# New durations and due times for the planner of a fused attention and two-MoE kernel

## The chip, the core and the metric

The kernel runs on one core of a Trainium2 chip. The metric is the time of one execution on the device in microseconds (us), as the median of several runs. The core has five engines with a queue each, which work in the order of their own queue and wait for one another by semaphores: TensorE (PE, matrix products into PSUM), VectorE (DVE), ScalarE (ACT), GpSimd (POOL) and SyncE (SP), which here only issues DMA transfers.

## The reference

Three layers one after the other, all in float32.

```python
# 1. a linear attention with decay, batch 4, 8 heads, 768 positions, head 32, state 16, in chunks
L  = exp(cum[i] - cum[j]) * (i >= j)          # cum: running sum of log(a) in the chunk
y  = ((C @ B.T) * L) @ x + (C @ state) * exp(cum)
state = exp(cum[-1]) * state + sum_j B_j x_j exp(cum[-1] - cum_j)
x  = y.transpose(0, 2, 1, 3).reshape(3072, 256)
# 2. first MoE: 256 -> 1536 -> 256
xn = x / sqrt(mean(x*x) + 1e-6) * rms_g
x  = (silu(xn @ w_gate) * (xn @ w_val)) @ w_out
# 3. second MoE: 256 -> 1024 -> 256
h  = x @ w_in
s  = h * softmax(h)
x  = (s - mean(s)) / sqrt(var(s) + 1e-6) * g_ln @ w_out
```

## The kernel before

**Units and blocks.** The 3072 tokens are 24 units of 128, and six blocks (0 to 5) of four units each. Attention goes unit by unit, the first MoE block by block, the second MoE unit by unit. Weights come as 64-bit numbers and are turned into float32 on the chip: 26 pieces of 512 KB, each loaded (`wl`), put together by three VectorE operations (`wc`, lines 114, 117, 120), and split into a high half (`wh`, ScalarE, line 127) and a low half (`w`, line 131). Every large product runs as three matmuls on such halves (high by high, low by high, high by low).

**Names.** An operation is named by its kind and by its unit `u` or by its block and slice `b.f` (12 slices of the 1536 inner columns). For attention: `lpe` (decay by PE, first four units), `cb` (C times B), `mt` (times L), `bw` (B scaled), `y` (the product of the unit, line 358 on), `s2` and `sbd` (new state), `sq`, `ms`, `ts`, `pw`, `rb` (RMS norm), `xc`, `xn`, `xh`, `xl` (input of the first MoE in halves). First MoE: `gm` and `vm` (gate and value, line 622), `th`, `si`, `mu` (SiLU and product), `ah`, `al` (halves), `o0` and `o1` (product with w_out, line 664, two halves of the 256 outputs), `x2h` and `x2l` (lines 673, 677: the block's result in halves). Second MoE: `h` (line 473), `mx`, `ex`, `so` (softmax times h), `tr`, `ds`, `dl` (transposed on VectorE in 32x32 squares, stored to DRAM, loaded back as `tt`), `tc` and `tl` (halves `uth` and `utl`, lines 573 and 578), `f` (product with w_out, line 602), `out` and `st` (result scaled and stored). For units 20 to 23, the tail, PE transposes instead.

**The planner.** None of this is written in its final order. Each operation is declared by `op(name, engine, us, due, function, after, new, use)`: its engine, a duration, a due time, the operations that must come before it, and the buffers it takes. `plan()` (line 994 on) goes forward in a clock of its own: for each engine it estimates when each ready operation could start, lets those within `SLACK` of the earliest compete, and takes the one with the lowest due time. Operations with `alt` may move from VectorE to GpSimd. The order it ends with is the order of each engine's queue; the chip knows nothing of durations or due times. Buffers are rings (`BUFS`): an operation can't take one before its last user is done. The two banks of `hc` serve both `cb` and `h`, in turn.

**Due times.** `PRO` and `FIRST` say when block 0 starts and how long it lasts, `per1`, `perA`, `per2` how long the other blocks last per unit. From these come `start[b]`, the due times of the gate and value products, of attention (`Y0`, `YPOS`, `YSPAN`), of weights (`wdue`, `WGAP`) and of the second MoE (`HLAG`, `TAILGAP`).

Of the kernel before, what the change touches and what calls it, by code (L numbers as in the profile page):

```python
# [38 lines left out]
NPE = 4  # L39
MARGIN = {"PE": 0.5}  # L40
CROW = 30.0
WGAP = 8.0
HLAG = (50.0, 26.0)
# [7 lines left out]
def fused_kernel(ctx, tc, aT, xbt, bcT, wg, wv, wo1, rg, wi2, wo2, gl, consts, out):  # L51
# [606 lines left out]
    def o_mm(b, f, m):  # L658
# [4 lines left out]
        for i, (aa, ww) in enumerate(((d["ah"], wo1_s[0]), (d["al"], wo1_s[0]), (d["ah"], wo1_s[1]))):  # L663
# [40 lines left out]
    per1, perA, per2 = 12.4, 2.7, 6.5  # L704
# [15 lines left out]
    for i in range(26):  # L720
        t = wdue(i)
        kind, c = pieces[i][0]
        op(f"wl{i}", "SP", 0.45, EARLY[i] if i < len(EARLY) else t - 6, (w_load, i), after=[f"wl{i-1}"] if i else [], new=[("u", f"st{i}")], kb=512)
# [8 lines left out]
        op(f"wh{i}", "ACT", 0.63, t, (w_hi, i), after=[f"wc{i}.2"], use=[f"wt{i}"])  # L732
        op(f"w{i}", "DVE", 0.68, t, (w_lo, i, V), after=[f"wh{i}"], use=[f"wt{i}"], lock=True)
# [15 lines left out]
    for u in range(NU):  # L749
# [53 lines left out]
        if u >= SPLIT:  # L803
            op(f"cb{u}", "PE", 0.5, Y - 12.0, (at_cbr, u), after=cbok + Lok[1], new=[("hc", f"pcb{u}")],
# [30 lines left out]
    for b in range(NB):  # L835
# [3 lines left out]
        for f in range(NF):  # L839
# [12 lines left out]
            op(f"mu{s}", "DVE", v_us(N), t, (g_mul, b, f), after=[f"si{s}", f"vm{s}"], use=[f"th{s}", f"pv{s}"])  # L852
# [25 lines left out]
    for u in range(NU):  # L878
# [115 lines left out]
    def plan():  # L994
# [48 lines left out]
        while len(order) < len(ops):  # L1043
# [138 lines left out]
```

## Time and profile before

| | |
|---|---|
| median of 3 timed runs | 558.02 us (557.35 to 560.51) |
| the profiled execution | 554.45 us, span 552.6 us |
| mean granted TensorE clock | 0.981 |
| PE busy | 524.9 us (95%) |
| VectorE busy | 422.8 us (77%) |
| ScalarE busy | 309.5 us (56%) |
| GpSimd busy | 117.7 us (21%) |

The span runs from the first to the last instruction; 1.85 us lie around it. Matmuls overlap, so the busy time of PE also holds time in which it starts them more slowly than it could. An idle time matters only on the engine that sets the end of its stretch. The granted clock is a share of full speed: 1.00 is 2.4 GHz and about 0.5 is 1.2 GHz.

### The profile page before, as it was taken

The numbers are of one execution on the slowest core, as the hardware profiler recorded it, in microseconds if no ns is written. First come the engines' busy times: TensorE is split into PE (matmuls) and PEld (weight loads), VectorE is DVE, ScalarE is ACT, GpSimd is POOL, SyncE is SP. The second block draws the span as 40 slices with busy tenths as digits, with TensorE's granted clock in tenths as the row PEclk, the third lists the DMA queues.
The fourth block names the chain that finished last, engine by engine and source line by source line (L and its number), as shares of the span: only waits on it lengthen the run. The fifth ranks groups of instructions, "written<-read, shape, count | busy, mean of one in ns | idle before, by whom it ended". The sixth has DMA issues, their size and how long they took to land.

```text
span 552.6 us, 9279 instructions
## 1 busy us (share of the span) xinstructions
PE 524.9 (95%) x3240; PEld 438.2 (79%) x3240; DVE 422.8 (77%) x802; ACT 309.5 (56%) x670; POOL 117.7 (21%) x140
## 2 busy tenths in 40 slices
PE   8869998999999999999999999999999799999886
PEld 8847876777788888888888878878888688887786
DVE  4887999999996898778887878877875565375674
ACT  6526655565675675566674665765643343344455
POOL 1522443550320120424112212013302000010000
PEclk9868999999999999999999999999999899999999
DMA  5664755561174252363353264242221221022200
GB/s 169 182 194 148 232 186 187 180 191 57 46 219 144 86 178 91 105 185 108 104 167 105 80 184 134 92 148 93 56 86 49 77 79 55 11 76 87 85 21 28
DMA packets 44014, 65.00 MB, mean 118 GB/s; under 512 B 7360, under 2 KB 30272, under 8 KB 43968
## 3 DMA queue, kind: packets, MB, share of 16 engines
q1 hardware_dynamic: 43968, 64.42, 37.2%
q8 instruction: 25, 0.41, 0.3%
q14 instruction: 21, 0.17, 0.1%
HBM read 50.57 MB, written 13.83 MB: 117 GB/s over the span
## 4 chain that ended last, share of the span: by engine, by line
PE 64%; DVE 20%; DMA 7%; issue 4%; ACT 3%; SPq 2%; POOL 0%; DVEq 0%; ACTq 0%; POOLq 0%
PE pv L622 12%; PE pg L622 12%; PE po L664 11%; PE pf L602 11%; PE ph L473 10%; DMA xb<-in_xbt_dram 3%; DVE wt L117 3%; DVE wt L120 2%; DMA tt<-scr 2%; DVE th L644 2%; DVE th L640 2%; DVE al L656 2%; PE y L363 2%; DVE utl L578 2%; PE y L358 1%
## 5 line engine op out<-in xcount | busy, mean ns | idle before, releaser
L650 ACT ACTIVATE ah<-th 128x512 fp32r<-128x512 f32 x72 | 45.3, 629 | 61.9 <-PE po L664 38.2
L656 DVE TENSOR_TENSOR al<-th,ah 128x512 fp32r<-128x512 f32 x61 | 45.2, 740 | 25.7 <-ACT ah L650 25.4
L640 DVE SCALAR_TENSOR_TENSOR th<-th,pg 128x512 f32<-128x512 f32 x72 | 49.2, 684 | 18.5 <-ACT th L636 17.9
L622 PE MATMUL pg<-xh,wg_h 128*128 128x512 f32 x144 | 60.7, 421 | 2.7 <-DVE th L640 1.3
L664 PE MATMUL po<-ah,wo_h 128*128 128x512 f32 x144 | 58.9, 409 | 0.0
L664 PE MATMUL po<-al,wo_h 128*128 128x512 f32 x144 | 56.7, 393 | 2.2 <-DVE al L656 2.2
L622 PE MATMUL pv<-xh,wv_h 128*128 128x512 f32 x144 | 58.4, 406 | 0.2 <-DVE th L644 0.2
L622 PE MATMUL pg<-xl,wg_h 128*128 128x512 f32 x144 | 57.4, 399 | 0.4 <-DVE xl L442 0.4
L622 PE MATMUL pg<-xh,wg_l 128*128 128x512 f32 x144 | 57.0, 396 | 0.0
L622 PE MATMUL pv<-xl,wv_h 128*128 128x512 f32 x144 | 56.8, 394 | 0.0
L622 PE MATMUL pv<-xh,wv_l 128*128 128x512 f32 x144 | 56.8, 394 | 0.0
L664 PE MATMUL po<-ah,wo_l 128*128 128x512 f32 x144 | 56.7, 394 | 0.0
L602 PE MATMUL pf<-wo_h,utl 128*128 128x256 f32 x176 | 50.8, 289 | 5.4 <-DVE utl L578 5.4
L644 DVE TENSOR_TENSOR th<-pv,th 128x512 f32<-128x512 f32 x72 | 49.7, 690 | 7.0 <-PE pv L622 1.2
L602 PE MATMUL pf<-wo_h,uth 128*128 128x256 f32 x176 | 50.3, 286 | 4.1 <-ACT uth L573 4.1
L227 ACT ACTIVATE L<-L,cneg 128x128 f32<-128x128 f32 x160 | 50.5, 390 | 5.3 <-DMA L<-crow 5.1
L636 ACT ACTIVATE th<-pg 128x512 f32<-128x512 f32 x72 | 42.6, 592 | 17.8 <-PE pg L622 17.3
L602 PE MATMUL pf<-wo_l,uth 128*128 128x256 f32 x176 | 50.2, 285 | 0.0
L538 POOL TENSOR_TENSOR sc<-sc,mhalf 128x1 f32<-128x1 f32 x24 | 13.5, 564 | 169.3 <-DVE sc L533 165.2
L602 PEld LDWEIGHTS pf<-wo_h,utl 128*128 128x128 f32 x176 | 34.4, 195 | 7.4 <-DVE utl L578 6.7
L602 PEld LDWEIGHTS pf<-wo_h,uth 128*128 128x128 f32 x176 | 33.9, 192 | 5.7 <-ACT uth L573 5.0
L473 PE MATMUL ph<-wi_h,xh 128*128 128x512 f32 x96 | 37.9, 395 | 0.2 <-DVE L L298 0.2
(151 smaller groups left out, 1225.8 us busy)
## 6 DMA issues: line engine op xcount, KB each, us to landing
L<-crow SPq DMA_DIRECT2D x20, 512.0 KB
scr<-dt SPq DMA_DIRECT2D x20, 512.0 KB
tt<-scr SPq DMA_DIRECT2D x80, 128.0 KB
bc<-in_bcT_dram SPq DMA_DIRECT2D x48, 128.0 KB
stage<-in_wo_dram SPq DMA_DIRECT2D x10, 512.0 KB
xb<-in_xbt_dram SPq DMA_DIRECT2D x24, 192.0 KB
stage<-in_wg_dram SPq DMA_DIRECT2D x6, 512.0 KB
stage<-in_wv_dram SPq DMA_DIRECT2D x6, 512.0 KB
```

The lines of the kernel that those rows point to most:

```text
L117: V.scalar_tensor_tensor(out=t, in0=v[:, :, 1], scalar=-0x40000000, in1=t, op0=ALU.bitwise_and, op1=ALU.bitwise_or)
L227: A.activation(d["L"][:, h], d["L"][:, h], AF.Exp, bias=cneg[:, u * 8 + h:u * 8 + h + 1])
L473: T.matmul(ph[c], xx[:, kk, k * P:(k + 1) * P], ww[:, kk, 512 * c:512 * c + 512], start=(i == 0), stop=(i == 5))
L538: G.tensor_tensor(out=sc[:, 7:8], in0=sc[:, 6:7], in1=mhalf, op=ALU.pow)
L602: T.matmul(d["pf"][:, 0:DM], uu[:, k], ww[:, k], start=(k == 0 and i == 0), stop=(k == 7 and i == 2))
L622: T.matmul(ps[:, :n], ww[:, kk, f * P:(f + 1) * P], xx[:, kk, :n], start=(i == 0), stop=(i == 5))
L636: A.activation(d["th"], d["pg"], AF.Tanh, scale=0.5)
L640: V.scalar_tensor_tensor(out=d["th"], in0=d["th"], scalar=1.0, in1=d["pg"], op0=ALU.add, op1=ALU.mult)
L644: V.tensor_tensor(out=d["th"], in0=d["pv"], in1=d["th"], op=ALU.mult)
L650: A.activation(d["ah"], d["th"], AF.Copy)
L656: e.tensor_tensor(out=d["al"], in0=d["th"], in1=d["ah"].bitcast(F32), op=ALU.subtract)
L664: T.matmul(po[b, m][:, :n], ww[:, f, m * P:(m + 1) * P], aa, start=(f == 0 and i == 0), stop=(f == NF - 1 and i == 2))
```

## The change

It has three parts. The declared durations are set to other numbers (a few hundredths to a few tenths of a us each), and so is the planner's estimate of a DMA's end. An operation that moves to GpSimd is now entered under its new engine, so that what follows it on VectorE is estimated as waiting for it. And the due times change: those of blocks, attention (with an offset per block, `YO`), second MoE (offset `HO`), and weights, among them `LEAD`, by which loads are due 0.49 us after their piece instead of 6 before. The raw pieces of the first MoE's w_out (`wraw`) now lie in the space of the second MoE's w_out until that is filled. There is new code for blocks under `WIDE`; as `WIDE` is 0, no block takes it.

```diff
+LEAD = -0.49
+PER = (12.2, 2.89, 5.7)
+WIDE = 0
-PRO = 34.0
-FIRST = 63.0
+PRO = 30.4
+FIRST = 69.8
-Y0 = (9.0, 4.0)
-YPOS, YSPAN = 0.65, 1.0
-TAILGAP = 5.0
-SLACK = 0.1
-SLACK0 = 0.1
+Y0 = (8.6, 3.8)
+YPOS = 0.55
+YSPAN = 0.72
+TAILGAP = 1.67
+SLACK = 0.02
+SLACK0 = 0.0
-EARLY = (-1.0, 1.5, 4.0, 6.0)
+EARLY = (-1.0, 1.5, 4.0, 3.2)
-CROW = 30.0
-WGAP = 8.0
-HLAG = (50.0, 26.0)
+CROW = 43.0
+WGAP = 10.3
+HLAG = (36.3, 16.4)
+YO = (0.0, 15.1, 1.41, -3.1, 3.9)
+HO = (-0.73, 5.6, -11.1, 0.0, -2.51, 0.0)
...
-            V.scalar_tensor_tensor(out=t, in0=v[:, :, 0], scalar=29, in1=t, op0=ALU.logical_shift_right,
+            raw = w_raw(i) if pieces[i][0][0] == "o" else t
+            V.scalar_tensor_tensor(out=raw, in0=v[:, :, 0], scalar=29, in1=t, op0=ALU.logical_shift_right,
...
-    per1, perA, per2 = 12.4, 2.7, 6.5
+    per1, perA, per2 = PER
...
-        op(f"wl{i}", "SP", 0.45, EARLY[i] if i < len(EARLY) else t - 6, (w_load, i), after=[f"wl{i-1}"] if i else [], new=[("u", f"st{i}")], kb=512)
+        op(f"wl{i}", "SP", 0.45, EARLY[i] if i < len(EARLY) else t - LEAD, (w_load, i), after=[f"wl{i-1}"] if i else [], new=[("u", f"st{i}")], kb=512)
...
+            t = gdue(WIDE, 2 * c + LAG) - 8.0
...
-            Y = start[b - 1] + (k + YPOS) * (start[b] - start[b - 1]) / n * YSPAN
+            Y = start[b - 1] + (k + YPOS) * (start[b] - start[b - 1]) / n * YSPAN + YO[b - 1]
...
-        alt(f"bw{u}", 0.42, (at_bw, u, G))
+        alt(f"bw{u}", 0.57, (at_bw, u, G))
-                op(f"lpe{u}.{g}", "PE", 0.9, Y - 5, (at_lpe, u, g), new=[(tg, f"pl{u}.{g}")], use=[f"pl{u}.{g}"],
+                op(f"lpe{u}.{g}", "PE", 1.15, Y - 5, (at_lpe, u, g), new=[(tg, f"pl{u}.{g}")], use=[f"pl{u}.{g}"],
...
+        H += HO[b]
...
-            op(f"f{u}.3", "PE", mm_us(DM, 24), H + 1, (m_f4, u), after=[f"tl{u}.1"] + wout, new=[(tt[0], f"pf{u}")],
+            op(f"f{u}.3", "PE", 24 * 0.118, H + 1, (m_f4, u), after=[f"tl{u}.1"] + wout, new=[(tt[0], f"pf{u}")],
...
-                o = ops[nm] = dict(o, us=o["alt"][0], fn=o["alt"][1])
+                o = ops[nm] = dict(o, e=e, us=o["alt"][0], fn=o["alt"][1])
...
-                end[nm] = dma_free + 1.0
+                end[nm] = max(dma_free, t + o["us"] + 0.6) + 1.2
```

The order that comes out of it differs at many places. Three of them follow. PE at the startup, between C times B of unit 1 and that of unit 2 (`y_214` is unit 0, `y_292` unit 1; `pg` and `pv` are the two groups of unit 2's decay). Before:

```order
L398 MATMUL y_214<-ones_77,sq_247 128x1 x2
L249 MATMUL pg_266<-um_73,la_79 128x128 x4
L249 MATMUL pv_278<-um_73,la_79 128x128 x4
L358 MATMUL y_292<-cd_167,sbd_261 128x128 x2
L363 MATMUL y_292<-L_205,xb_164 32x128 x8
L368 MATMUL y_292<-xb_164 32x64 x4
L420 MATMUL y_214<-ident_74,r_272 128x128
```

And now:

```order
L268 MATMUL pg_260<-um_73,la_79 128x128 x4
L417 MATMUL y_214<-ones_77,sq_255 128x1 x2
L268 MATMUL pv_279<-um_73,la_79 128x128 x4
L377 MATMUL y_292<-cd_165,sbd_253 128x128 x2
L382 MATMUL y_292<-L_206,xb_143 32x128 x8
L387 MATMUL y_292<-xb_143 32x64 x4
L439 MATMUL y_214<-ident_74,r_286 128x128
```

The first decay group of unit 2 moved ahead of unit 0's sum of squares (`ms`).

VectorE at the end of block 4: `utl` is the low half for f of unit 14, `sc`, `ut` and `dt` behind the maximum (`TENSOR_REDUCE`) are those of unit 15, `xl` by line 677 is block 4's result. Before:

```order
L640 SCALAR_TENSOR_TENSOR th_4735<-th_4735,pg_4712 128x512
L644 TENSOR_TENSOR th_4735<-pv_4728,th_4735 128x512
L533 SCALAR_TENSOR_TENSOR sc_4692<-sc_4692 128x1
L411 TENSOR_SCALAR r_4754<-y_4697 128x1
L656 TENSOR_TENSOR al_4766<-th_4735,ah_4760 128x512
L484 TENSOR_REDUCE sc_4790<-ph_4768 128x1
L431 SCALAR_TENSOR_TENSOR xts_4724<-xts_4724,rgt_75,y_4697 128x128 x2
L677 SCALAR_TENSOR_TENSOR xl_4796<-po0_4132,xh_4795 128x512
L507 SCALAR_TENSOR_TENSOR ut_4800,sc_4790<-ph_4768,ut_4800 128x1024
L578 TENSOR_TENSOR utl_4804<-tt_4781,uth_4803 128x4x8x32
L442 TENSOR_TENSOR xl_4178<-xts_4724,xh_4177 128x2x128
L555 STREAM_TRANSPOSE dt_4811<-ut_4800 128x8x4x32
```

And now:

```order
L662 SCALAR_TENSOR_TENSOR th_4760<-th_4760,pg_4742 128x512
L669 TENSOR_TENSOR th_4760<-pv_4753,th_4760 128x512
L597 TENSOR_TENSOR utl_4764<-tt_4730,uth_4763 128x4x8x32
L681 TENSOR_TENSOR al_4789<-th_4760,ah_4787 128x512
L503 TENSOR_REDUCE sc_4816<-ph_4774 128x1
L526 SCALAR_TENSOR_TENSOR ut_4818,sc_4816<-ph_4774,ut_4818 128x1024
L574 STREAM_TRANSPOSE dt_4831<-ut_4818 128x8x4x32
```

The low half of unit 14 moved ahead of all of unit 15, and block 4's result behind it.

PE at the end of block 5 (`po` is block 5's last pair of o products, `pf` f of unit 18, `ph` h of unit 20). Before:

```order
L664 MATMUL po0_4912<-ah_5370,wo1_l_88 128x512
L664 MATMUL po1_4918<-ah_5370,wo1_h_87 128x512
L664 MATMUL po1_4918<-al_5375,wo1_h_87 128x512
L664 MATMUL po1_4918<-ah_5370,wo1_l_88 128x512
L602 MATMUL pf_5418<-wo2_h_91,uth_5409 128x256
L602 MATMUL pf_5418<-wo2_h_91,utl_5410 128x256
```

And now:

```order
L692 MATMUL po0_4921<-ah_5429,wo1_l_88 128x512
L692 MATMUL po1_4970<-ah_5429,wo1_h_87 128x512
L692 MATMUL po1_4970<-al_5434,wo1_h_87 128x512
L692 MATMUL po1_4970<-ah_5429,wo1_l_88 128x512
L492 MATMUL ph_5461<-wi2_h_89,xh_5448 128x512
L492 MATMUL ph_5461<-wi2_h_89,xl_5449 128x512
```

The product f of unit 18 left the place between the last o and h of unit 20; it now stands before the last three pairs of o.

## Rows read from the trace of the kernel before

**Rows 1.** Windows: from:to, length, busy us (instructions) per engine, PEclk, DMA.
```profile
core 0: us, PE busy (x) PEld busy (x) DVE busy (x) ACT busy (x) POOL busy (x), PEclk, DMA share, GB/s
0.00:38.20 38.20, 30.37 (x286) 26.92 (x286) 27.08 (x63) 19.38 (x54) 13.40 (x23) 0.86 0.59 167
38.20:107.00 68.80, 65.55 (x411) 51.36 (x411) 62.69 (x116) 39.52 (x99) 25.21 (x26) 0.96 0.60 190
107.00:182.00 75.00, 72.67 (x444) 58.47 (x443) 67.82 (x121) 47.72 (x109) 20.76 (x23) 1.00 0.43 134
182.00:431.00 249.00, 247.60 (x1510) 208.29 (x1511) 192.43 (x362) 149.35 (x313) 52.08 (x59) 1.00 0.37 116
436.00:446.00 10.00, 9.66 (x47) 8.75 (x48) 4.85 (x11) 2.95 (x5) 0.55 (x1) 0.83 0.36 119
500.00:552.60 52.60, 42.79 (x270) 37.64 (x268) 30.68 (x78) 25.42 (x51) 3.26 (x6) 1.00 0.17 58
```

**Rows 2.** Waits of PE over the span: us in total, times, longest.
```profile
PE pf L602 <- DVE utl L578: 5.4, 5, 2.3
PE pf L602 <- ACT uth L573: 4.1, 2, 2.1
```

**Rows 3.** Timeline of PE, startup: start, us, instruction [idle before it, released by].
```profile
16.56 0.63 PE L398 MATMUL y<-ones,sq 128*128 128x1 f32 x4 [1.63 <-ACT xts L426]
17.05 2.06 PE L249 MATMUL pg<-um,la 128*128 128x128 f32 x8
20.53 0.61 PE L358 MATMUL y<-cd,sbd 128*128 128x128 f32 x4
38.23 0.80 PE L622 MATMUL pg<-xh,wg_h 128*128 128x512 f32 x1 [1.21 <-ACT xh L438]
```

**Rows 4.** Timeline of VectorE, startup.
```profile
15.88 0.22 DVE L377 COPY s<-y 128x64 f32<-128x64 f32 x1
```

**Rows 5.** Chain of waits, block 4: start, us, piece of work.
```profile
391.72 1.39 PE pg L622 x6
...
394.47 2.72 PE ph L473 x12
397.19 2.82 PE pf L602 x24
400.01 1.40 PE po L664 x6
```

**Rows 6.** Timeline of PE, f of unit 14; last row from the chain.
```profile
434.88 0.38 PE L602 MATMUL pf<-wo_h,uth 128*128 128x256 f32 x1 [2.03 <-ACT uth L573]
436.33 0.38 PE L602 MATMUL pf<-wo_h,utl 128*128 128x256 f32 x1 [1.08 <-DVE utl L578]
...
436.33 4.51 PE pf L602 x23
```

**Rows 7.** Timeline, unit 17: last matmul of h, and `utl`.
```profile
480.58 0.39 PE L473 MATMUL ph<-wi_l,xh 128*128 128x512 f32 x1
...
494.13 1.22 DVE L578 TENSOR_TENSOR utl<-tt,uth 128x1024 fp32r<-128x1024 f32 x1
```

**Rows 8.** Timeline of ScalarE at the end of block 4.
```profile
432.19 0.60 ACT L673 ACTIVATE xh<-po 128x512 fp32r<-128x512 f32 x1 [4.27 <-PE po L664]
```

**Rows 9.** Timeline of PE, tail: f of units 18 (two rows), 19 and 23.
```profile
512.16 0.38 PE L602 MATMUL pf<-wo_h,uth 128*128 128x256 f32 x1 [2.10 <-ACT uth L573]
513.62 0.38 PE L602 MATMUL pf<-wo_h,utl 128*128 128x256 f32 x1 [1.08 <-DVE utl L578]
527.23 0.39 PE L602 MATMUL pf<-wo_h,utl 128*128 128x256 f32 x1 [2.34 <-DVE utl L578]
542.30 0.39 PE L602 MATMUL pf<-wo_h,xh 128*128 128x256 f32 x1 [0.97 <-DVE xl L592]
```

**Rows 10.** Groups by line: instruction, count, busy us, mean ns, idle before it.
```profile
L677 DVE SCALAR_TENSOR_TENSOR xl<-po,xh 128x512 fp32r<-128x512 f32 x12 | 8.1, 682 | 0.1
L673 ACT ACTIVATE xh<-po 128x512 fp32r<-128x512 f32 x12 | 7.1, 590 | 10.8 <-PE po L664 10.7
```

**Rows 11.** Waits of SyncE's queue: us in total, times, longest.
```profile
SPq L568 <- DMA scr<-dt: 20.0, 10, 2.7
```

More of the change, by code (lines that the diff above doesn't have):

```diff
@@ L179, in p_hi @@
     def p_hi(c):
+        if not wo2_s:
+            wo2_s.extend(wp.tile([P, 8, DM], F32R, name=f"wo2_{s}", bufs=1) for s in "hl")
         A.activation(wo2_s[0][:, 4 * c:4 * c + 4], w2[c], AF.Copy)
@@ L614, in fused_kernel, with awtag @@
     po = {}
+    def awtag(f):
+        return ("ah", "al")[f % 2]
     def g_mm(b, f, ws, tag):
@@ L662, in o_mm @@
         d = act[b, f]
-        for i, (aa, ww) in enumerate(((d["ah"], wo1_s[0]), (d["al"], wo1_s[0]), (d["ah"], wo1_s[1]))):
+        if b < WIDE:
+            T.matmul(po[b, m][:, :n], w_raw(3 * (f // 2) + 2).bitcast(F32)[:, 256 * (f % 2) + m * P:256 * (f % 2) + (m + 1) * P], d["aw"], start=f == 0,
+                     stop=f == NF - 1)
+        for i, (aa, ww) in enumerate(() if b < WIDE else ((d["ah"], wo1_s[0]), (d["al"], wo1_s[0]), (d["ah"], wo1_s[1]))):
             T.matmul(po[b, m][:, :n], ww[:, f, m * P:(m + 1) * P], aa,
@@ L731, in fused_kernel @@
             continue
-        op(f"wh{i}", "ACT", 0.63, t, (w_hi, i), after=[f"wc{i}.2"], use=[f"wt{i}"])
-        op(f"w{i}", "DVE", 0.68, t, (w_lo, i, V), after=[f"wh{i}"], use=[f"wt{i}"], lock=True)
+        wu = [f"wt{i}"]
+        last = []
+        if kind == "o":
+            t = gdue(WIDE, 2 * c + LAG) - 8.0
+            wu = [f"raw{c // 4}"]
+            ops[f"wc{i}.2"]["new"] += [(f"wo2_{'hl'[c // 4]}", wu[0])] if c % 4 == 0 else []
+            ops[f"wc{i}.2"]["use"] += wu
+            last = [f"o{m}{b}.{2 * c + q}" for b in range(WIDE) for q in range(2) for m in range(2)]
+        op(f"wh{i}", "ACT", 0.63, t, (w_hi, i), after=[f"wc{i}.2"], use=wu)
+        op(f"w{i}", "DVE", 0.68, t, (w_lo, i, V), after=[f"wh{i}"] + last, use=wu, lock=True)
         alt(f"w{i}", p_us(512), (w_lo, i, G))
@@ L740, in fused_kernel @@
         op(f"psub{c}", "DVE", 1.22, t, (p_sub, c), after=["pmean"], use=["mean"], lock=True)
-        op(f"phi{c}", "ACT", 1.06, t, (p_hi, c), after=[f"psub{c}"], use=["w2h", "w2l"])
+        op(f"phi{c}", "ACT", 1.06, t, (p_hi, c), after=[f"psub{c}"], use=["w2h", "w2l"],
+           new=[] if c else [("wo2_h", "w2H"), ("wo2_l", "w2L")])
         op(f"plo{c}", "DVE", 1.22, t, (p_lo, c), after=[f"phi{c}"], use=["w2h", "w2l"], lock=True)
@@ L803, in fused_kernel @@
         if u >= SPLIT:
-            op(f"cb{u}", "PE", 0.5, Y - 12.0, (at_cbr, u), after=cbok + Lok[1], new=[("hc", f"pcb{u}")],
+            op(f"cb{u}", "PE", 0.48, Y - 12.0, (at_cbr, u), after=cbok + Lok[1], new=[("hc", f"pcb{u}")],
                use=[f"bh{u}", f"cb{u}", f"pcb{u}"])
@@ L844, in fused_kernel @@
             wg_n, wv_n, wo_n = ([f"wh{3*(f//2)+q}", f"w{3*(f//2)+q}"] for q in range(3))
-            op(f"gm{s}", "PE", mm_us(N, 6), t, (g_gate, b, f), after=ready + wg_n + pr, new=[("pg", f"pg{s}")],
+            op(f"gm{s}", "PE", mm_us(N, 6) + 0.03, t, (g_gate, b, f), after=ready + wg_n + pr, new=[("pg", f"pg{s}")],
                use=[f"pg{s}", f"xs{b}"])
-            op(f"vm{s}", "PE", mm_us(N, 6), t, (g_val, b, f), after=[f"gm{s}"] + wv_n, new=[("pv", f"pv{s}")],
+            op(f"vm{s}", "PE", mm_us(N, 6) + 0.015, t, (g_val, b, f), after=[f"gm{s}"] + wv_n, new=[("pv", f"pv{s}")],
                use=[f"pv{s}", f"xs{b}"])
@@ L851, in fused_kernel @@
             op(f"si{s}", "DVE", v_us(N), t, (g_silu, b, f), after=[f"th{s}"], use=[f"th{s}", f"pg{s}"])
-            op(f"mu{s}", "DVE", v_us(N), t, (g_mul, b, f), after=[f"si{s}", f"vm{s}"], use=[f"th{s}", f"pv{s}"])
+            wide = b < WIDE
+            op(f"mu{s}", "DVE", v_us(N), t, (g_mul, b, f), after=[f"si{s}", f"vm{s}"], new=[(awtag(f), f"aw{s}")] if wide else [],
+               use=[f"th{s}", f"pv{s}"] + ([f"aw{s}"] if wide else []))
+            for m in range(2) if wide else ():
+                op(f"o{m}{s}", "PE", mm_us(N, 4), to, (o_mm, b, f, m), after=[f"mu{s}", f"wc{3*(f//2)+2}.2"] + ([f"o{m}{b}.{f-1}"] if f else []) + ([f"o0{s}"] if m else []),
+                   new=[(f"po{m}", f"po{m}{b}")] if f == 0 else [], use=[f"aw{s}", f"po{m}{b}", f"raw{f // 8}"])
+            if wide:
+                continue
             op(f"ah{s}", "ACT", a_us(N, 0.02), t + 2, (g_ah, b, f), after=[f"mu{s}"], new=[("ah", f"ah{s}")],
@@ L891, in fused_kernel @@
         if not tl:
-            op(f"h{u}.1", "PE", mm_us(512, 12), H, (m_h2, u), after=x2ok + win, new=[("hc", f"ph{u}")],
+            op(f"h{u}.1", "PE", mm_us(512, 12) + 0.02, H, (m_h2, u), after=x2ok + win, new=[("hc", f"ph{u}")],
                use=[f"ph{u}", f"x2{b}"])
```

38 lines of the change are left out of this document (25 added, 13 removed).

## The prediction
> **What bounds the kernel now.** I read the stretches first [rows 1]: the reader is to look at the first two numbers of each row, its length and TensorE's (PE's) busy time. From 182 to 431 us PE is busy 247.60 of 249.00 us: there only PE counts, and an order can win 1.4 us at most. Elsewhere PE stands: 7.8 us of the first 38.2, 3.3 of the next 68.8 (block 0, where VectorE is busy 62.69 us too), 2.3 up to 182, 9.8 of the last 52.6. Next, for whom PE waits [rows 2]: 5.4 us for the low and 4.1 us for the high half of the transposed activations of the second MoE (`utl`, `uth`), the operands of its last product f. Both kernels issue the same matmuls, so the change can only add or remove waits, and time at half clock behind them.
>
> **Startup (0 to 38.2 us), -2.4 us.** In [rows 3] the product ms of unit 0 sits until 16.56, since ScalarE's copy comes after VectorE's state copy s2, which only ran at 15.88 [rows 4] behind weight conversions. Queued behind ms on PE are the two groups of unit 2's decay product; they then take from 17.05 to 20.53, 3.5 us, and unit 1's y starts at 20.53. The changed order puts the first of these groups ahead of ms and gives unit 1's B scaling, which stood ahead of s2, to GpSimd. So that group starts as soon as PE is free, 1.6 us of wait (16.56's row) is filled with it, and y can start when VectorE is ready, some 3 us sooner. Not all of that arrives at the first gate matmul (38.23): VectorE does more before y of unit 3 (one low half of the weights and a state mask that GpSimd did, unit 1's `xl`), and the last `xl` stands behind three small operations instead of one. Ends: -4 (all of it and 1 us of the later waits), +0.5 (all lost on VectorE). I take -2.4, nearest the 3 us that the row shows. The slow clock of the first gate products (0.96 is the mean granted over block 0 [rows 1], 1.00 later) stays: they still follow a startup full of waits.
>
> **Block 0 and the first half of block 1 (38 to 182), -2.5 us.** Here conversions, gate and value all want VectorE. By counts of its instructions times their median durations, block 0 holds the same VectorE work in both orders; only places move. The second products o come one step later, which spares waits such as 2.2 us for one `al`. PE's idle time, 3.3 and 2.3 us [rows 1], is the most that goes; the same amount may come if VectorE falls behind at another place. I take -2.0 and -0.5; ends -5.6 and +5.
>
> **Blocks 2 to 4 (182 to 431), 0.** Ends -1.4 (all idle time) and +4 (below, the slower rival).
>
> **Unit 14, at the end of block 4 (432 to 441), -4.6 us.** What a matmul group costs is in [rows 5]: gate, value and a pair of o products 1.4 each, h 2.72, f 2.82. What unit 14 waited for is in [rows 6]: PE sat 2.03 us for `uth` and 1.08 for `utl`, and behind that f ran its 23 matmuls in 4.51 us against 2.82 for 24: 1.69 us, at a granted clock of 0.83 over 436 to 446 [rows 1]. Sum 4.8. The transposition takes its time whatever happens: in unit 17, where nothing stood in its way, 14.4 us from the end of the last h matmul (480.97) to the end of `utl` (495.35) [rows 7]. For unit 14 the old order leaves PE only four pairs of o (5.6), one gate and value (2.8) and h of unit 15 (2.7): 11.1 us and one small y. ScalarE was no help: it sat 4.27 us behind the copy of block 4's result, which waits for o [rows 8], with `uth` queued behind it. In the new order, between h and f of unit 14 lie f of 13 (2.82), three gates and values (8.25), three pairs of o (4.2) and h of 15 (2.72): 18.0 us, and VectorE has `utl` ahead of unit 15's maximum, where it stood behind its maximum, product and `xl` (second excerpt). 18.0 against 14.4 to 17 leaves nothing to wait for. I take -4.6; it is 0 if the chain grows to 21 us.
>
> **Tail (500 to the end), -4.0 us.** PE waits in [rows 9]: f of 18 2.10 and 1.08, f of 19 2.34, f of 23 0.97. Unit 18 had f of 17 (2.82), a gate and value (2.75), four pairs of o (5.6), h of 19 (2.72): 13.9 us; it gets 18.0. Unit 19's `utl` is now ahead of unit 21's maxima on VectorE and its `uth` no longer behind unit 18's. So 5.5 us go. But in the old order f of 18 lay between the last o and h of unit 20, and now nothing does (third excerpt): PE stands until ScalarE and VectorE have copied block 5's result, 0.59 + 0.68 us [rows 10] and about 0.2 for handing over, 1.5 us. That wait is bounded by 0.7 (first half only) and 3.0 (with a clock loss like unit 14's). It also gives unit 19 room: 2.82 + 4.2 + 1.5 + 8.2 (three units' h) = 16.7 us before its f. The last 0.97 I leave. -5.5 + 1.5 = -4.0; ends -6.5 and -1.
>
> **A rule against this.** After unit 14's waits the clock fell (0.83), after unit 18's, 3.18 us in all, the stretch stayed at 1.00 [rows 1, 9]. The Trainium skill, "TensorE: Matmul & The Clock Gate", section "HAM oscillation — how this bites in real kernels", says that gaps in TensorE's work send it back to half rate, so that what follows starts cold. The trace agrees in one of two like places. By the rule the new wait before h of 20 costs its 1.5 us and a cold start; by the row of unit 18 the 1.5 alone.
>
> **The sum.** -2.4 - 2.5 + 0 - 4.6 - 4.0 = -13.5. The profiled execution took 554.45 us (span 552.6), so 541.0 for its like. The three timed runs have a median of 558.02, 3.6 above it; carried over: **544.5 us**.
>
> **Rivals.**
> 1. *The waits only move.* Startup and block 0 are held by VectorE, which has the same work, and the f waits partly reappear before h of 20 and f of 22. Then unit 14's 4.6 us alone go: 553.4. For it: VectorE's 62.69 busy us of 68.8 in block 0. Against: the f of 14 and 18 now have more PE work before them than the chain takes.
> 2. *It does not do what it says.* Same work, same PE bound for 249 of 552 us; gains and new waits cancel: 556 to 560. For it: in 249 of the 552 us PE is busy but for 1.4. Against: the 9.5 us of [rows 2] lie outside that stretch.
> 3. *Cold after the new wait.* As forecast, but h of 20 starts at half clock (price 1.7, unit 14's row): 546. This is the rule above as a mechanism of this kernel; PE fell to half clock in one of two such waits.
> 4. *Slower: SyncE's queue in blocks 2 to 4.* The transposition goes out and back through SyncE, in order. The new order puts other transfers and the store of the unit before, which waits for that unit's f, ahead of the load back. If the load of each of the 14 units 6 to 19 leaves 2 us later, the distances of 17 to 20 us no longer hold a chain that takes 14.4 at its best, and each f waits about 1.5: +21 us on the 544.5 gives 565. It decides from 1 us a unit, where the gain is gone. For it: SyncE waited 20.0 us in 10 loads back for the store before them, 2.7 at the longest [rows 11]. Against: the old order, too, has the store of the unit before in that place, and PE still lost only 1.4 us in these blocks.
>
> **How the numbers follow.** Forecast 0.55, rival 3 0.12, rival 1 0.19, rival 2 0.08, rival 4 0.06. "Faster" means under 555.2, "slower" over 560.8 (0.5%, about what a measurement can tell from no change). Faster: 0.55 + 0.12 + 0.19 = 0.86; same 0.08; slower 0.06. The forecast's own range, from about half of each part's ends, is 538 to 551. Range 536 to 555: below, all gains at their ends (-4 - 5.6 - 1.4 - 4.8 - 6.5 = -22 gives 536); above, rival 1 with a little more lost.
>
> **What would show it.** Right: no wait of PE for `uth` or `utl` over 1 us in units 14, 18 and 19; one new wait of `ph` for `xl` of about 1.5 us before unit 20; the first gate matmul near 36; the 0.83 after 436 gone. The startup step is wrong if the first gate matmul starts after 38; the unit 14 and tail steps if f still waits; block 0 if it takes over 69 us from the first gate matmul to block 1's. The forecast as a whole falls if PE's idle time between block 2 and block 4 grows beyond 4 us.

## The result, and the profile after

The changed kernel takes 542.70 us (median of 4 runs, 542.03 to 542.93), the kernel before 557.98 (557.35 to 560.51): ratio 0.9716, 95% interval 0.9685 to 0.9747. The forecast was 544.5. Profiled executions: 554.45 before, 542.93 after, span 541.2.

To compare the two orders at the same work, I took for each operation on TensorE (PE) its start, less the durations that all groups before it have when nothing waits [rows 5]: that is the time PE has lost so far. The difference of the two kernels' lost time, by stretch:

| stretch (us, before) | forecast | measured |
|---|---|---|
| startup, to the first gate product | -2.4 | -0.6 |
| 38 to 182 | -2.5 | +2.1 |
| blocks 2 to 4 | 0 | -2.8 |
| unit 14 | -4.6 | -5.2 |
| tail | -4.0 | -5.0 |
| sum | -13.5 | -11.5 |

The windows of the changed kernel, as [rows 1]:

```profile
0.00:37.65 37.65, 29.83 (x287) 26.29 (x287) 26.50 (x65) 19.43 (x54) 13.66 (x21) 0.87 0.59 171
37.65:108.10 70.45, 67.14 (x407) 52.03 (x407) 64.90 (x117) 39.34 (x101) 20.30 (x21) 0.92 0.59 191
108.10:182.00 73.90, 72.08 (x438) 58.33 (x439) 71.32 (x129) 45.95 (x106) 18.94 (x20) 1.00 0.36 114
182.00:431.00 249.00, 248.95 (x1537) 210.91 (x1536) 191.87 (x358) 152.56 (x319) 51.34 (x65) 1.00 0.38 121
436.00:446.00 10.00, 10.00 (x46) 8.13 (x45) 6.56 (x9) 4.20 (x7) 0.28 (x1) 1.00 0.18 54
490.00:541.20 51.20, 46.56 (x283) 40.27 (x281) 30.70 (x75) 24.91 (x51) 2.74 (x5) 0.99 0.14 47
```

From 182 to 431 us PE stands for 0.05 us where it stood for 1.4, and the stretch after 436 has its full clock (0.83 before). Block 0 is longer (70.45 against 68.8) at a lower clock (0.92 against 0.96), with VectorE busy 2.2 us longer and GpSimd 4.9 us less.

Waits of PE over the span, as [rows 2]: us in total, times, longest.

```profile
PE y L439 <- POOL r L435: 2.3, 1, 2.3
PE pg L644 <- DVE wg_l L148: 2.0, 2, 1.4
PE pg L644 <- DVE th L662: 1.8, 3, 1.3
...
PE pg L644 <- ACT xh L457: 1.5, 1, 1.5
...
PE ph L492 <- ACT xh L701: 0.4, 1, 0.4
PE pf L621 <- DVE utl L597: 0.4, 1, 0.4
PE ph L492 <- DVE xl L705: 0.2, 1, 0.2
```

The 9.5 us for `uth` and `utl` are down to 0.4, and the new wait before h of 20 (`ph` for `xh` and `xl` of block 5) is 0.6. What is left at the top are waits of the startup and of blocks 0 and 1. Unit 14, from the chain of waits, as [rows 6]:

```profile
425.89 2.77 PE ph L492 x12
428.67 2.82 PE pf L621 x24
431.49 1.39 PE pg L644 x6
```

f of 14 follows h of 15 at once and takes its 2.82. SyncE's queue waited for the store before a load back about as often as before [rows 11], and from 182 to 431 us it cost PE nothing (0.05 us of idle time):

```profile
SPq L587 <- DMA scr<-dt: 21.6, 12, 3.5
```

### The profile page after: what moved, and what is told of

It is laid out like the page before. It is cut to its first block, busy times and chain, and to the rows that moved or that the text cites. A ratio compares the mean times of both kernels' runs of the same rounds, so it can differ in the third digit from the quotient of the medians.

```text
span 541.2 us, 9289 instructions
## 1 busy us (share of the span) xinstructions
PE 523.6 (97%) x3240; PEld 437.6 (81%) x3240; DVE 424.5 (78%) x806; ACT 308.3 (57%) x670; POOL 109.2 (20%) x136
## 4 chain that ended last, share of the span: by engine, by line
PE 85%; DVE 10%; issue 2%; ACT 1%; DMA 1%; SPq 0%; POOL 0%; DVEq 0%; ACTq 0%; POOLq 0%
PE pg L644 17%; PE pv L644 17%; PE po L692 16%; PE pf L621 13%; PE ph L492 12%; PE y L382 2%; PE pcb L310 2%; PE y L377 1%; DVE wt L128 1%; PE pcb L362 1%; DVE L L320 1%; DMA bc<-in_bcT_dram 1%; PE y L417 1%; DVE wt L131 1%; DVE th L662 1%
## 5 line engine op out<-in xcount | busy, mean ns | idle before, releaser
L681 DVE TENSOR_TENSOR al<-th,ah 128x512 fp32r<-128x512 f32 x60 | 41.7, 695 | 19.8 <-ACT ah L675 19.5
L621 PE MATMUL pf<-wo_h,utl 128*128 128x256 f32 x176 | 49.6, 282 | 0.4 <-DVE utl L597 0.4
L516 ACT ACTIVATE ut<-ph,sc 128x1024 f32<-128x1024 f32 x20 | 22.3, 1114 | 34.3 <-DVE sc L503 34.3
L250 POOL TENSOR_SCALAR_AFFINE_SELECT L<-L 128x1024 f32<-128x1024 f32 x20 | 23.0, 1148 | 83.7 <-ACT L L246 73.9
```

Source lines behind the costliest of these rows:

```text
L250: G.affine_select(out=d["L"], in_=d["L"], pattern=[[0, 8], [1, P]], base=0, channel_multiplier=-1, compare_op=ALU.is_ge, fill=0.0)
L516: A.activation(d["u"], ph[0], AF.Exp, bias=sc[:, 0:1], accum_out=sc[:, 1:2])
L621: T.matmul(d["pf"][:, 0:DM], uu[:, k], ww[:, k], start=(k == 0 and i == 0), stop=(k == 7 and i == 2))
L681: e.tensor_tensor(out=d["al"], in0=d["th"], in1=d["ah"].bitcast(F32), op=ALU.subtract)
```

## The experiments

But for the three that change the planner, each kernel is the one before or the changed one, with a helper behind `plan()` that moves the named operations to another place in their own engine's queue (in 11 and 12 some low halves to GpSimd's) and leaves the rest. The indented text under an edit is what was expected before the run.

**1. Unit 14 by distance alone (from the kernel before).**

```diff
+("f14.3", "after", "vm5.1"), ("h16.1", "after", "f14.3"), ("f15.3", "after", "o15.1"),
+("th5.1", "before", "tc15.1"), ("out14", "after", "th5.1"),
+("si5.1", "before", "mx16.0"), ("mu5.1", "before", "mx16.0")
```

> The kernel before, with nothing but unit 14's distance on TensorE changed: f of 14 moves behind two more gates and values (5.5 us), h of 16 behind it, f of 15 behind one more gate, value and pair of o; ScalarE and VectorE are moved only so far that nothing waits in a circle. Theory A (distance is what unit 14 lacked): f of 14 no longer waits (2.03 and 1.08 before), no half clock behind it (1.69), block 4 to 5 shorter by 4.8, time 553.2 (552.5 to 554). Theory B (the wait only moves, as the new place of f lets the load back of unit 15 stand where f of 15 needs it): f of 15 waits for 2 to 3 us instead, 556 to 557.

565.54 (561.7 to 567.62, ratio 1.0125, 1.0086 to 1.0165): slower than either theory allows. f of 14 does not wait any more, but the first gate product of block 5, now ahead of it, does. PE and ScalarE in this run:

```profile
435.51 0.49 PE L622 MATMUL pg<-xh,wg_h 128*128 128x512 f32 x1 [2.34 <-ACT xh L438]
437.00 0.50 PE L622 MATMUL pg<-xl,wg_h 128*128 128x512 f32 x1 [1.00 <-DVE xl L442]
```

```profile
432.52 0.60 ACT L673 ACTIVATE xh<-po 128x512 fp32r<-128x512 f32 x1 [4.27 <-PE po L664]
434.10 1.05 ACT L573 ACTIVATE uth<-tt 128x1024 fp32r<-128x1024 f32 x1
435.05 0.41 ACT L438 ACTIVATE xh<-xts 128x256 fp32r<-128x256 f32 x1
```

`xh` of unit 23 stands behind block 4's copy on ScalarE, as `uth` does. The old wait for `uth` had covered that. So distance on PE is not enough: whatever PE does instead must not need what is queued behind that copy. More was lost later, behind the moves of this experiment itself: 1.84 us for an `ah` behind `uth` of 15 and 3.04 for a `th` behind a variance. So the 565.54 is not the price of distance alone.

**2. Unit 14 by the queues alone (from the kernel before).**

```diff
+("tc14.1", "before", "x2h4.0"), ("tl14.1", "before", "mx15.0")
```

> The kernel before, with TensorE's order kept, and only the two halves of unit 14 moved up: uth ahead of the copy of block 4's result on ScalarE, utl ahead of unit 15's maximum on VectorE. The load back of unit 14 landed at about 432.2, so uth ends at 433.4 and utl at 434.6, 1.7 earlier. Theory A (distance): f of 14 still waits, about 0.6 and 1.0, so -1.7, or -3.4 if the clock stays up; 554.6 to 556.3. Theory B (the places on ScalarE and VectorE were the whole cause): no wait is left, -4.8, 553.2. Theory C (unit 15's maximum, now 3 us later, costs what unit 14 gains): 557.5 to 559.

555.73 (ratio 0.9951, 0.9924 to 0.9977): -2.6, within theory A. PE at f of 14 and the gate product behind it:

```profile
431.12 0.38 PE L602 MATMUL pf<-wo_h,uth 128*128 128x256 f32 x1 [0.34 <-ACT uth L573]
432.38 0.38 PE L602 MATMUL pf<-wo_h,utl 128*128 128x256 f32 x1 [0.88 <-DVE utl L578]
...
436.35 0.50 PE L622 MATMUL pg<-xl,wg_h 128*128 128x512 f32 x1 [0.78 <-DVE xl L442]
```

2.0 us of wait stay, since the distance is still 11 us, and nothing runs at half clock behind them (granted 1.00 from 429 to 440 us). f of unit 15, which did not wait before, now waits 0.65 us for its `utl`, so a part of theory C came too. The queues alone give about half of what unit 14 lost; the distance alone, as it was moved in experiment 1, only moved the wait.

**3. f of unit 18 back as a cover (from the changed kernel).**

```diff
+("f18.3", "after", "o15.11"), ("out18", "after", "x2h5.1"), ("st18o", "after", "dl19"),
+("ah5.11", "before", "ex19.0"), ("al5.11", "before", "mx19.0")
```

> The changed kernel, with f of unit 18 back in its old place, between the last o product and h of unit 20 (its result's copy and store behind block 5's copy and unit 19's load back; the halves ah and al of the last slice ahead of unit 19's maximum, so that o needn't wait for them). Theory A (the new wait before h of 20 costs what the sum said, 1.5, or what the trace of the changed kernel shows, 0.4 + 0.2 idle and about 0.6 of slower matmuls): f covers the copy and 0.6 to 1.5 go, 541.2 to 542.1 against 542.7. Theory B (the wait moves: h of 19 to utl of 19 is a chain of its own): f of 19 waits for utl longer by what h of 20 won, 542.5 to 543.

546.32 (ratio 0.9768, 0.9741 to 0.9794), 3.6 above the changed kernel: both theories fall. The trace, PE at h of 20, then ScalarE:

```profile
509.86 0.60 PE L492 MATMUL ph<-wi_h,xh 128*128 128x512 f32 x1 [2.45 <-ACT xh L701]
```

```profile
508.08 1.15 ACT L543 ACTIVATE ut<-ut,sc 128x1024 f32<-128x1024 f32 x1 [2.62 <-DVE sc L538]
509.23 1.06 ACT L701 ACTIVATE xh<-po 128x512 fp32r<-128x512 f32 x2
```

Block 5's copy does not wait for o (its last product ended at 504.58) but stands behind unit 19's variance (L543), which waits for unit 19's chain on VectorE. That chain runs later here, because the experiment also moved `ah` and `al` of the last slice ahead of it (the exponential of unit 19 starts at 504.26, in the changed kernel at 500.75); so the run says nothing of f of 18 as a cover by itself. In the changed kernel the variance (505.17 to 506.32) happens to end as o does (506.56). The copy was named rightly as what h of 20 waits for, and wrongly as waiting for o alone.

**4 to 6. The change taken apart.** The changed kernel with the old due times, constants and slacks (`durations`); with the old durations, DMA estimate and counting (`due`); the kernel before with the counting alone (`count`):

```diff
-                o = ops[nm] = dict(o, us=o["alt"][0], fn=o["alt"][1])
+                o = ops[nm] = dict(o, e=e, us=o["alt"][0], fn=o["alt"][1])
```

> The changed kernel with all due times, their constants and slacks as before; what stays of the change are the declared durations, the estimate of a DMA's end, the counting of moved operations and the place of the raw w_out pieces. In the order that comes out, between h and f of unit 14 lie 18.3 us of TensorE work (12.8 before, 18.4 in the changed kernel), with uth and utl behind block 4's copy as before; units 18 and 19 keep 13.9 and 12.6; the decay group stands ahead of unit 0's mean of squares. Theory A (a wait goes where its own distance grows): unit 14's 4.6 and the startup's 0.6 go, the tail's waits stay: about 553 against 558. Theory B (distance alone moves the wait, as in the run with spacing alone): 557 to 562. Theory C (the durations carry the whole gain): 543 to 546.

560.70 (ratio 1.0034, 1.0001 to 1.0067). At unit 14 f does not wait, although `uth` and `utl` stand behind block 4's copy as before; PE waits 0.45 us for `xl` of unit 23 and loses 1.0 in all instead of 5.4. Here `xh` of unit 23 had also come ahead of block 4's copy, which is what experiment 1 lacked. The tail's waits for f of 18 stayed, with a clock of 0.77 from 515 to 530 us. And before block 1 PE sat, at a granted clock of 0.71 from 105 to 118 us:

```profile
113.47 1.01 PE L417 MATMUL y<-ones,sq 128*128 128x1 f32 x4 [4.38 <-DVE s L398]
...
117.29 0.79 PE L644 MATMUL pg<-xh,wg_h 128*128 128x512 f32 x1 [1.39 <-ACT xh L457]
```

Theory A reads the two places rightly and the time wrongly.

> The changed kernel with the declared durations, the estimate of a DMA's end and the counting of moved operations as before; what stays are the due times, their constants and slacks, and the place of the raw pieces. In its order unit 14 has 16.8 us between h and f, with utl ahead of most of unit 15's work, unit 18 has 23.6, unit 19 has 12.6; the startup on TensorE is the old one. Theory A (places at the block ends carry the gain, whatever the durations): unit 14's 4.6 and unit 18's 3.2 go, unit 19 still waits 2 to 3: 548 to 551. Theory B (due times only fit the new durations): 554 to 560.

548.02 (ratio 0.9797, 0.9772 to 0.9823), as theory A has it, though f of 19 waited only 0.37 us. So the due times alone bring 10.4 of the 15.3 us; the durations alone, with the DMA estimate and the counting, lose 2.3, and on top of the due times they bring 5.3. The place of the raw pieces was the new one in both runs; none parted it.

> The kernel before with one line of the change: an operation moved to GpSimd is entered under GpSimd. No operation changes its place on any engine by it alone. Theory A: the same time as before (558), and its profile is a second profile of the old order; if the old order loses time at random at half clock, its profile differs from the first one (552.6 span) at the places behind waits, and its runs spread over several us as those of before do. Theory B (the first profile was typical, and 3.6 us lie outside the span): the same span again, 552 to 553.

559.56 (ratio 1.0004, 0.9979 to 1.0030), 556.47 to 560.61; its profiled execution 556.47, span 554.8: theory A. Two executions of the same order, f of unit 18 behind the same waits (2.10 us for `uth` in both, then 1.08 and 0.88 before the first product with `utl`), first in the kernel before, then here, with the windows:

```profile
513.62 2.97 PE pf L602 x23
...
510.00:535.00 25.00, 19.48 (x123) 17.26 (x123) 18.18 (x44) 13.38 (x26) 0.55 (x1) 1.00 0.17 53
```

```profile
513.36 5.26 PE pf L602 x23
...
510.00:535.00 25.00, 19.90 (x105) 17.70 (x106) 16.04 (x40) 10.97 (x23) 0.55 (x1) 0.86 0.15 53
```

Whether the clock falls behind a wait differs between executions; here it is worth 2.3 us.

**7 and 8. The end of the startup (from the changed kernel).** VectorE there, in the changed kernel, with PE's last three starts:

```profile
32.88 0.60 DVE L450 SCALAR_TENSOR_TENSOR xts<-xts,rgt,y 128x128 f32<-128x128 f32 x2
33.44 0.28 DVE L398 SCALAR_TENSOR_TENSOR s<-s,e,y 128x64 f32<-128x64 f32 x1
...
34.10 0.15 DVE L430 TENSOR_SCALAR r<-y 128x1 f32<-128x1 f32 x1
```

```profile
32.73 0.61 PE L417 MATMUL y<-ones,sq 128*128 128x1 f32 x4 [0.57 <-ACT xts L445]
35.66 0.48 PE L439 MATMUL y<-ident,r 128*128 128x128 f32 x1 [2.33 <-POOL r L435]
37.65 0.79 PE L644 MATMUL pg<-xh,wg_h 128*128 128x512 f32 x1 [1.51 <-ACT xh L457]
```

PE's sum of squares of unit 3 ends at 33.34, but VectorE takes it (`r`, 34.10) behind what is queued there.

```diff
+("s23", "before", "xn2"), ("ts3", "before", "xn2"), ("xl3", "after", "xn3")
```

> The changed kernel, with the end of the startup on VectorE reordered: state of unit 3 and its mean of squares ahead of unit 2's xn, and unit 3's xl directly behind its xn, ahead of three other operations. Theory A (VectorE's order ate the startup's gain): the mean is ready 0.6 us earlier, xh of unit 3 no longer waits for the copy behind xn (0.4), and the first gate product doesn't wait for xl: it starts at about 36.7 instead of 37.65 and block 0 ends 1.0 to 1.5 earlier, 541.2 to 541.7. Theory B (block 0 is held by VectorE, an earlier start is lost there): the first gate product starts earlier, but block 1 starts as before, 542.5 to 543.

542.36 (ratio 0.9720, 0.9686 to 0.9754): just under theory B's times, and no change that the interval can tell. `r` comes earlier (rb3 at 34.76), but xn of 3 still stands behind the rest of VectorE's queue, and the first gate product starts at 37.49, block 1's at 107.47 (108.13 in the changed kernel).

```diff
+("xn2", "before", "wc4.1"), ("ts3", "before", "wc4.1"), ("s23", "before", "wc4.1"), ("xl2", "before", "wc4.1"),
+("sbd3", "before", "wc4.1"), ("xn3", "before", "wc4.1"), ("xl3", "before", "wc4.1"), ("wh4", "after", "xh3")
```

With that `wc4.1`, `wc4.2`, `cc0`, `w4`, `cc1`, `bw5` and `wc5.0` stand behind `xl3`.

> The changed kernel, with weight piece 4 (last two steps, low half) and the copies that stood before unit 3's xl put behind it on VectorE, and its high half behind unit 3's xh on ScalarE. Theory A (VectorE's queue at the end of the startup ate the gain): unit 3's xn no longer stands behind 2.5 us of other work, the first gate product starts at about 35.9 instead of 37.65, and the time is 541 against 542.7. Theory B (the work only moves into block 0, where VectorE is full): the first gate product starts at 35.9, but block 1 starts at 108 as before, 542.5 to 543.5. Theory C (the stage buffer of piece 4 is free 5 us later, so its successor's load is late): block 0 is longer than the start is earlier, over 543.5.

543.21 (ratio 0.9727, 0.9694 to 0.9760). Now `xh` of 3 is ready at 35.3, and the gate still starts at 37.54, since its PSUM bank holds a product that `cc0` (L1002), one of the moved operations, must copy out:

```profile
37.54 0.77 PE L644 MATMUL pg<-xh,wg_h 128*128 128x512 f32 x1 [3.42 <-DVE ct L1002]
```

None of the three theories had this.

**9 to 11. Block 0 (from the changed kernel).** Its largest wait, gate 0.10: PE, then VectorE, then GpSimd.

```profile
95.16 0.50 PE L644 MATMUL pg<-xh,wg_h 128*128 128x512 f32 x1 [0.52 <-ACT wg_h L144]
...
97.25 0.80 PE L644 MATMUL pg<-xh,wg_l 128*128 128x512 f32 x1 [1.35 <-DVE wg_l L148]
```

```profile
94.37 1.50 DVE L128 TENSOR_SCALAR wt<-stage 128x512 int32<-128x512 int32 x1
...
96.50 0.68 DVE L148 TENSOR_TENSOR wg_l<-wt,wg_h 128x512 fp32r<-128x512 f32 x1
```

```profile
94.07 1.50 POOL L681 TENSOR_TENSOR al<-th,ah 128x512 fp32r<-128x512 f32 x1 [0.17 <-ACT ah L675]
```

The low half of piece 15 stands behind the first steps of piece 16, and the first of them takes 1.50 us beside GpSimd's `al` where it mostly takes 0.42.

```diff
 # 9
+("wc15.2", "before", "xl6"), ("w15", "before", "wc16.0")
 # 10: those of 9, and
+("wh15", "before", "e1x8")
 # 11: those of 10, and with these three by GpSimd
+("w12", "before", "bw7"), ("w14", "before", "ls8"), ("w17", "before", "ls9")
```

> The changed kernel, with two VectorE operations of block 0 moved: the last step of weight piece 15 ahead of xl of unit 6, and the low half of piece 15 ahead of the first step of piece 16. In the changed kernel the gate product 0.10 took 4.16 us from its start instead of 1.39, for this low half, and the o products behind it ran at half clock. Theory A (only the place is wrong): 2.6 us of wait go and about 0.9 behind it, block 0 falls from 70.5 to 67 to 68, time 539.2 to 540.2 against 542.7. Theory B (VectorE's work as a whole bounds block 0): the wait comes back at the next slices, 542 to 543.

544.27 (ratio 0.9741, 0.9708 to 0.9774): the high half of piece 15 stood behind an `ah` on ScalarE, so gate 0.10 still took 3.53. The time is above both theories, by no more than the interval.

> The changed kernel, with weight piece 15 early on all engines: its last step on VectorE ahead of xl of unit 6, its high half on ScalarE ahead of e1 of unit 8, its low half on VectorE directly behind the product of slice 0.9, so that it ends before GpSimd's al of 0.9 begins (in the run that moved VectorE alone, the high half stood behind ah of 0.9 and the low half took 1.42 beside that al). Theory A (one piece's place costs block 0 its time): gate 0.10 takes 1.4 (4.16 in the changed kernel, 3.53 in that run), and 2.5 go from block 0, 540.2 against 542.7; if the clock stays up from 90 to 110 (0.82 and 0.84 in the changed kernel), 3.3 more. Theory B (VectorE bounds block 0): gate 0.10 is served, but the next wait for VectorE grows, 542 to 544.

541.65 (ratio 0.9697, 0.9666 to 0.9728; the changed kernel's interval overlaps it). Gate 0.10 is served and takes 1.66, and PE then waits for the next thing from VectorE, by way of ScalarE's copy, which waits for VectorE's state copy. PE, then ScalarE:

```profile
99.77 0.61 PE L417 MATMUL y<-ones,sq 128*128 128x1 f32 x4 [1.82 <-ACT xts L445]
```

```profile
99.34 0.38 ACT L445 ACTIVATE xts<-y 128x256 f32<-128x256 f32 x1 [2.66 <-DVE s L398]
```

That state copy, at 99.03, stands behind a step of piece 16 that took 1.68 us beside GpSimd's `al`. Block 0 takes 70.2, as theory B has it; the time lies a little under its 542 to 544.

> The changed kernel with weight piece 15 early on all engines (as in the run of that name) and, besides, the low halves of pieces 12, 14 and 17 on GpSimd instead of VectorE. In block 0 the kernel before has 7 low halves on VectorE and 7 on GpSimd, the changed kernel 9 and 4. Theory A (block 0 got longer because VectorE got more work): VectorE has 2.0 us less in block 0, and block 0 takes 68.5 to 69 instead of 70.2 to 70.5; 540 to 541 against 542.7. Theory B (what GpSimd takes over slows VectorE's operations beside it by as much): block 0 stays at 70 to 70.5, 541.5 to 542.7. Theory C (half clock behind any wait sets block 0's length): 70 or more, with the granted clock under 0.9 in 80 to 110.

542.67 (ratio 0.9715, 0.9684 to 0.9746), block 0 69.7, VectorE busy 64.26 there against 64.55 in the run before it: between A and B. Of the 2.0 us that left VectorE, all but 0.3 came back: about 0.8 as its operations beside GpSimd's took longer (a step of piece 13 took 1.64 beside the low half of 12), and 0.7 since one more `mu` now runs before block 1 begins.

**12. Together.** The startup of 8 with `cc0` and `cc1` ahead of piece 4, block 0 of 10 with the low half of 14 on GpSimd, and the tail:

```diff
+("x2h5.0", "before", "va19"), ("x2h5.1", "before", "va19"), ("tl19.1", "before", "so20.0")
```

> The changed kernel with what the runs so far point to. Startup: piece 4 and the later copies behind unit 3's xl on VectorE, but the copy cc0, whose bank the first gate product takes, ahead of it (in the run that moved piece 4, xh of unit 3 was ready at 35.3 and the gate then sat 3.4 us for cc0). Block 0: piece 15 early on all engines, the low half of piece 14 on GpSimd. Tail: block 5's copy ahead of unit 19's variance on ScalarE, utl of unit 19 ahead of unit 20's products on VectorE. Theory A: the first gate product starts at 35.5 (37.65), block 0 keeps 70, the waits of 0.4 before h of 20 and f of 19 go: 539 to 540 against 542.7 of the changed kernel. Theory B (VectorE paces block 0): the first gate starts at 35.5, block 1 at 108 as before, and only the tail's 0.5 to 0.8 remain: 541 to 542.

546.84 (ratio 0.9811, 0.9779 to 0.9842): slower than the changed kernel. PE:

```profile
35.73 0.50 PE L644 MATMUL pg<-xh,wg_h 128*128 128x512 f32 x1 [1.25 <-ACT xh L457]
43.21 0.64 PE L644 MATMUL pg<-xh,wg_h 128*128 128x512 f32 x1 [2.63 <-DVE th L662]
...
510.07 0.50 PE L492 MATMUL ph<-wi_h,xl 128*128 128x512 f32 x1 [2.12 <-DVE xl L705]
```

The start came out as expected (35.73), and the second gate product gave it all back, as `th` of the first stands on ScalarE behind piece 5, now late. In the tail the copy passed the variance on ScalarE, but on VectorE the operation that waits for the variance still stood ahead of `xl`, which cost 2.12 us and half clock in h of 20 (4.14 us from its start to its second half's instead of 1.4; 0.62 granted from 510 to 514.4). No version beats the changed kernel by more than the interval.

## Why the prediction was right, and where it was wrong

**Unit 14 (-4.6, measured -5.2): right in size, and its reason was right but not whole.** The step gave the distance as the cause and the queues as a help. Experiment 4 bears out the distance: there f of 14 waits for nothing, with `uth` and `utl` where the old queues had them. What the step left out is `xh` of unit 23, which the new order also puts ahead of block 4's copy on ScalarE: where it stays behind, distance only moves the wait to it (experiment 1). The queues alone leave 2.0 us (experiment 2).

**Tail (-4.0, measured -5.0): right in its parts, and 1.0 short.** f of 18 waits no more, f of 19 0.4 us; by lost time that is -5.4 (forecast -5.5). The new wait before h of 20 was put at 1.5. It shows as 0.6 us of standing, but between block 5's last product o and h of 21 PE lost 1.2 us; why that wait was no longer is not as thought (experiment 3). The rest, -0.9, is the end, which the step left alone: the wait of 0.97 before f of 23 [rows 9] is 0.16 now, before f of 22. Rival 3, cold behind the new wait, did not happen here: 0.99 over the tail. It is a true rival, though: in experiments 3 and 12, where the wait was 2.45 and 2.12, h of 20 ran at half clock (0.64 and 0.62). The Trainium skill, "TensorE: Matmul & The Clock Gate", section "HAM oscillation — how this bites in real kernels", has gaps in TensorE's work end in a cold start; the traces agree in some executions and not in others with the very same wait (1.00 and 0.86 in experiment 6's pair).

**Startup (-2.4, measured -0.6): the step failed at "some 3 us sooner".** Only one of the two decay groups moved; `ms` and the other group still stand ahead of y of unit 1, so the 1.63 us of wait [rows 3] was all that could be filled, not 3. Of that little came: y of unit 1 started at 20.25 instead of 20.53. C times B of unit 1, just ahead, took 1.81 us with 0.62 granted (1.16 in the kernel before, at 1.00), so half of the gap was gone when the moved group came (15.82 instead of 14.93), and what followed ran at half clock (0.53 over 14 to 20 us; the kernel before has 1.00 over 14 to 17 and 0.51 over 17 to 20.5). Why the clock fell earlier no run shows. At the end of the startup VectorE's queue, not PE's order, set the first gate product (experiments 7, 8 and 12: moved there it starts at 35.73). That was named as a loss and priced too low.

**Block 0 and after (-2.5, measured +2.1): the step failed at "only places move".** The count that it rests on holds. VectorE's operations that start between the first gate product and block 1's come to 66.5 us in the old order and 66.4 in the new, each taken at the median duration of its kind. But VectorE is busy 64.90 us there against 62.69 [rows 1], because its operations took longer: five of the old order ran over 0.1 us longer than that median, 3.2 us together, seven of the new one 5.3 us. Each of the twelve began while a GpSimd operation was running, though GpSimd does less in the new order (it has 4 low halves where it had 7). Others that began so, most of them with an operand in PSUM, took their usual time; no run had the block without GpSimd's work. Three of the kinds, before and after (instructions, total us, mean ns; those that only end in the stretch count too):

```profile
L114 DVE TENSOR_SCALAR wt<-stage 128x512 int32<-128x512 int32 x14 | 5.9, 421 | 0.0
L240 DVE TENSOR_TENSOR cd<-cd,e 128x128 f32<-128x128 f32 x1 | 0.8, 810 | 0.0
L131 DVE TENSOR_TENSOR wv_l<-wt,wv_h 128x512 fp32r<-128x512 f32 x4 | 2.7, 684 | 0.0
```

```profile
L128 DVE TENSOR_SCALAR wt<-stage 128x512 int32<-128x512 int32 x14 | 8.1, 577 | 0.0
L259 DVE TENSOR_TENSOR cd<-cd,e 128x128 f32<-128x128 f32 x2 | 2.3, 1136 | 0.0
L148 DVE TENSOR_TENSOR wv_l<-wt,wv_h 128x512 fp32r<-128x512 f32 x1 | 1.5, 1503 | 0.0
```

So what the forecast left out is which operations would run beside each other. From the first gate product to block 1's, the four profiles of the old order take 68.8 to 69.5 us at a clock of 0.95 to 0.96; the eight of the new order with its due times and durations 69.7 to 73.1 at 0.89 to 0.93. Shown: one wait mended brings the next one (experiment 10), and an earlier start is lost in this block (experiment 12). Open: how much of the 2 us is VectorE's longer operations and how much half clock behind its waits, since no run parted them.

**Blocks 2 to 4 (0, measured -2.8).** The step allowed 1.4 us, all of PE's idle time. But a wait cost more here than the idle time that its row shows. In the kernel before, three products with a wait inside (f of unit 1, the first gate product of block 4, f of unit 11) took 0.95, 0.66 and 0.63 us longer than their like without one, 2.2 us together, of which their rows show 1.27 as idle:

```profile
182.32 0.38 PE L602 MATMUL pf<-wo_h,utl 128*128 128x256 f32 x1 [0.69 <-DVE utl L578]
349.01 0.50 PE L622 MATMUL pg<-xl,wg_h 128*128 128x512 f32 x1 [0.38 <-DVE xl L442]
373.90 0.39 PE L602 MATMUL pf<-wo_h,utl 128*128 128x256 f32 x1 [0.20 <-DVE utl L578]
```

None of them waits in the changed kernel. Rival 4, SyncE's queue, did not come.

**The sum and the carry.** Between profiled executions the terms came to -11.5, 2.0 less than forecast: startup and block 0 came out as rival 1 had it, and worse (+1.5 instead of -4.9), and the other places gave 4.4 more than forecast. The 3.6 us carried from the profiled execution to the median were right for the kernel before only: its runs in all the comparisons lie between 554.5 and 561.8, and both profiles of its order (554.45, 556.47) at the lower end, while the changed kernel's four lie within 0.9 us and its profiled one is the longest. The errors offset each other; that the forecast came within 1.8 us is luck, but the two places that bring most of the gain, unit 14 and the tail, were the right ones. That the old order's spread is half clock behind its waits is shown for one place (2.3 us, `count`), not for all of it.

## What to carry to other kernels

Before moving an operation away from a wait, list what the same slow queue releases next: the operation put in its place may need that too. "The same work in both orders" can hold by count and fail in time: ask also which operations will now run beside one that slows them. On an engine that is 90% busy a mended wait can bring the next one, as in experiment 10.

## What was not expected of the hardware

The same order with the same waits ran f of 18 in 2.97 or 5.26 us: the granted clock fell in one execution (0.86 over 25 us) and not in the other (1.00).

A VectorE step of 0.42 us took 1.50 when it began in GpSimd's `al` (94.07 to 95.57) and ended at 95.87, shortly after it. The Trainium skill, "SBUF — State Buffer", section "SBUF: two separate sides", says that VectorE and GpSimd share a pair of ports by an exclusive lock, so that the one that starts second waits out the other's whole instruction; it says so of VectorE operations in a two-port mode, or with two inputs in SBUF beside a GpSimd operation that reads SBUF. The rows fit it, though none shows whether this step, which has one input, ran in such a mode: each of the twelve slowed operations of block 0 began second, and `mt` of unit 7, which reads PSUM and one tile of SBUF, took its usual time (two operations, 84.02 to 85.30) beside a low half on GpSimd (84.11 to 85.39).
